# A gated linear attention and a squared-ReLU feed-forward: operand pairs of scaled float16 in place of float32r

## The chip, the cores and the metric

The kernel runs on one core of a Trainium2 chip. A core has a matrix engine (PE, with its weight loads shown apart as PEld), a vector engine (DVE), an activation engine (ACT), GpSimd (POOL) and a sync engine (SP), which here issues most DMAs. The metric is the device time of one execution in microseconds (us).

## The reference

A linear attention with a per-channel forget gate gives `x` of 3072 tokens by 384; a feed-forward with a squared ReLU takes it up to 2048 and back to 384. All in float32.

```python
f = 1.0 / (1.0 + np.exp(-f_logit))                  # B, H, S, D = 4, 8, 768, 48
for t in range(S):
    state = f[:, :, t, :, None] * state + einsum('bhd,bhe->bhde', k[:, :, t], v[:, :, t])
    y[:, :, t] = einsum('bhd,bhde->bhe', q[:, :, t], state)
x = y.transpose(0, 2, 1, 3).reshape(3072, 384)
h = x @ w_in                                        # 384 x 2048
g = np.maximum(h, 0.0) ** 2
out = g @ w_out                                     # 2048 x 384
```

## The kernel before

**Blocks.** The tokens are cut into 6 blocks of 512 (4 batches of 128 positions). For a block, the attention leaves three tiles `x[0..2]` of 128 rows by 512; each holds two parts, the value rounded to the matmul's number format and the rest. 24 units of attention (4 head pairs for each block) run ahead of the feed-forward blocks that need them.

**One feed-forward step.** The 2048 hidden rows are 16 groups `f` of 128. In step `f`, `up(f)` (L249) makes `h` in a PSUM bank `ph`: for each of 3 tiles of `x`, three matmuls of 128x128 by 512 (high by low, low by high, high by high), 9 in all. `square(f)` is three ACT instructions: ReLU (L259), square (L260), both in place, and a rounded copy `gh` (L261). `rest(f)` is one DVE instruction, `gl = ph - gh` (L266), after which the bank is free again. `down(f)` (L276) adds 9 matmuls into three PSUM banks `po`. `run` issues `up(n)`, `square(n)`, `rest(n)` and then `down(n - LAG)` with LAG = 2; the `ph` banks are two, in the last block three. So 96 steps issue 1728 matmuls of 512 columns (and 6 more for a fourth tile of the first block, `ys`).

**Order of the blocks.** Groups 0 to 7 of block 0 run first, between units of attention (the lists FIRST and SECOND, written out by hand, fix the order on every engine). Then come block 1 with all 16 groups, groups 8 to 15 of block 0, and blocks 2 to 5. `owed` is the last `down` and the eviction of the block before, done after the first `up` of the next. `hooks` hang further work at a step: decoding of weights during block 1 (`decode`: ACT copies the high halves, DVE puts the words together, ACT rounds them at L145, DVE makes the rest at L147), stages of attention for later blocks, DMA issues, and the sizes of the weights (`sizes`, L159, in blocks 2 and 3: an ACT sum of absolute values for each of the 32 weight tiles).

**Number format.** Both parts of `x`, of the weights and of `g` are float32r. Such a matmul is one instruction in the program and loads its own weights.

**The verdict.** `verdict` (L870) decides whether a general path must do the work over: it looks at the smallest decay (`low`) and at the weights' sizes (`sums`), turns the result by one PE transpose `pl` (L882) and leaves a flag, in block 4. In the last block at step 12 every engine loads the flag into a register; the branch stands after the last matmul, ahead of the last output DMAs. The general path is not taken with these inputs.

Of the kernel before, what the change touches and what calls it, by code (L numbers as in the profile page):

```python
# [42 lines left out]
LARGE = 2.0**120  # L43


LAG = 2
AHEAD = 4
# [20 lines left out]
VERDICT_AT = 12  # L68
# [15 lines left out]
class Moe:  # L84


    def __init__(self, ctx, tc, const, sums, out):
        self.tc, self.nc, self.sums, self.out = tc, tc.nc, sums, out

        self.const, self.w, self.row, self.ps, self.turns = const, {}, {}, {}, 0  # L90
        self.xs, self.w4, self.third_bank, self.heads = [], None, None, 0
# [101 lines left out]
    def hidden(self, ctx):  # L193
        self.gp = ctx.enter_context(self.tc.tile_pool(name="gp", bufs=3))
# [58 lines left out]
    def square(self, f):  # L253

        nc, ph = self.nc, self.ph[f]
        gh, gl = (
            self.gp.tile([P, NT], F32R, tag=t, name=f"{t}{self.blk}_{f}") for t in ("gh", "gl")
        )
        nc.scalar.activation(ph, ph, AF.Relu)  # L259
        nc.scalar.activation(ph, ph, AF.Square)  # L260
        nc.scalar.copy(out=gh, in_=ph)  # L261
        self.g[f] = gh, gl

    def rest(self, f):
# [15 lines left out]
    def run(self, hooks, obs=None, before=None):  # L280


        for n in range(len(self.fs) + LAG):
            if before and not obs and n == len(self.fs) + LAG - 1:
                return
            self.at = n
            if obs and n == len(self.fs):
                for e in range(NJ):
                    for f in self.fs[-LAG:]:
                        self.down(f, (e,))  # L290
                    for _, cs in tails(e):
                        self.nc.vector.tensor_copy(out=obs[e][:, cs], in_=self.po[e][:, cs])
# [15 lines left out]
            if n >= LAG:  # L308
                self.down(self.fs[n - LAG])
# [763 lines left out]
```

## Time and profile before

| | before |
|---|---|
| time, median of 3 runs (lowest to highest), us | 490.74 (490.41 to 490.92) |
| span of the profiled execution, us | 489.3 |
| PE / PEld / DVE / ACT / POOL busy, us | 471.9 / 377.5 / 248.9 / 284.3 / 29.7 |
| matmuls (as many weight loads) | 4775 |
| granted clock of PE, mean | 0.996 |

The page gives the span from the first to the last instruction; of the profiled execution no other time is given. The runs' median lies 1.4 us above the span. A busy time is the union of the instructions' stretches; matmuls overlap each other in it, so it says that PE has always something in flight, not that it streams at its full rate.

### The profile page before, as it was taken

How to read it: one execution, taken by the hardware profiler on the slowest of the kernel's cores; microseconds unless marked ns; L12 is line 12 of the kernel's file. 1: busy time of each engine (PE TensorE's matmuls, PEld its weight loads, DVE VectorE, ACT ScalarE, POOL GpSimd, SP SyncE). 2: the span in 40 equal slices, each digit the busy share in tenths (PEclk: the TensorE clock that was granted, in tenths of full speed). 3: DMA queues.
4: the chain of work that ended last, by engine and by line, in shares of the span. 5: the costliest groups of instructions: out<-in, count | busy, mean ns of one | idle time of the engine just before them, and what ended most of it. 6: DMA issues, size and time to landing. Idle time of an engine off the chain costs nothing.

```text
span 489.3 us, 11451 instructions
## 1 busy us (share of the span) xinstructions
PE 471.9 (96%) x4775; PEld 377.5 (77%) x4775; DVE 248.9 (51%) x456; ACT 284.3 (58%) x591; POOL 29.7 (6%) x66
## 2 busy tenths in 40 slices
PE   2889999999999999999999999999999999999996
PEld 2667777888788888888888788888888887888884
DVE  7999962678575365727335636434643322211112
ACT  4589874976755564656565665664745442534441
POOL 4411000000000000000000000000000000000000
PEclk9899999999999999999999999999999999999999
DMA  8888107582544525360423470134440001100002
GB/s 288 246 301 289 31 6 254 162 275 57 108 113 137 122 37 161 80 150 1 105 41 101 118 157 10 37 92 109 122 90 3 1 2 33 68 0 0 1 0 70
DMA packets 64748, 48.65 MB, mean 99 GB/s; under 512 B 46912, under 2 KB 50352, under 8 KB 64688
## 3 DMA queue, kind: packets, MB, share of 16 engines
q1 hardware_dynamic: 64096, 46.78, 34.6%
q0 software_dynamic: 448, 0.92, 0.9%
q8 instruction: 39, 0.64, 0.6%
q14 instruction: 21, 0.17, 0.1%
q10 hardware_dynamic: 144, 0.13, 0.1%
HBM read 35.22 MB, written 7.86 MB: 88 GB/s over the span
## 4 chain that ended last, share of the span: by engine, by line
PE 91%; DMA 5%; DVE 1%; ACT 1%; issue 1%; SPq 1%; POOL 0%; DVEq 0%; ACTq 0%
PE po L276 41%; PE ph L249 41%; DMA raw<-in_w_dram 3%; PE ds L561 2%; PE ds L550 2%; PE py L609 2%; DMA vn<-in_vN_dram 1%; PE ph L621 1%; PE ph L609 1%; PE py L621 1%; SPq L439 1%; DMA x<-ys 1%; DVE fkq L465 0%; ACT rx L487 0%; ACT ys L638 0%
## 5 line engine op out<-in xcount | busy, mean ns | idle before, releaser
L249 PE MATMUL ph<-x,w 128*128 128x512 f32 x864 | 218.2, 398 | 0.8 <-DVE sc L568 0.4
L249 PEld LDWEIGHTS ph<-x,w 128*128 128x128 f32 x864 | 161.6, 188 | 41.3 <-DMA x<-ys 1.2
L276 PE MATMUL po<-gh,w 128*128 128x512 f32 x576 | 180.9, 395 | 0.0
L266 DVE TENSOR_TENSOR gl<-ph,gh 128x512 fp32r<-128x512 f32 x96 | 66.4, 692 | 219.5 <-ACT gh L261 218.3
L259 ACT ACTIVATE ph<-ph 128x512 f32<-128x512 f32 x96 | 56.1, 585 | 147.6 <-PE ph L249 147.6
L276 PEld LDWEIGHTS po<-gh,w 128*128 128x128 f32 x576 | 108.3, 188 | 25.1
L276 PE MATMUL po<-gl,w 128*128 128x512 f32 x288 | 115.9, 402 | 0.0
L276 PEld LDWEIGHTS po<-gl,w 128*128 128x128 f32 x288 | 54.1, 188 | 13.9 <-DVE gl L266 0.7
L261 ACT CAST gh<-ph 128x512 fp32r<-128x512 f32 x96 | 56.4, 587 | 3.0
L260 ACT ACTIVATE ph<-ph 128x512 f32<-128x512 f32 x96 | 55.9, 582 | 3.0
L456 POOL TENSOR_SCALAR fkq<-fkq 128x8 f32<-128x8 f32 x18 | 12.3, 685 | 284.2 <-DVE fkq L451 124.3
L495 ACT COPY sx<-sp 48x208 f32<-48x208 f32 x44 | 16.1, 365 | 16.0 <-DVE sp L583 15.4
L451 DVE TENSOR_TENSOR_SCAN fkq<-fz,dr 128x520 f32<-128x520 f32 x18 | 22.2, 1232 | 2.1 <-ACT fz L446 2.1
L465 DVE TENSOR_TENSOR_SCAN fkq<-fz,dz 128x520 f32<-128x520 f32 x18 | 22.4, 1242 | 0.6
L609 PEld LDWEIGHTS py<-sc,vn 64*48 64x48 f32 (+1 forms) x384 | 16.2, 126 | 7.3 <-issue 7.3
L145 ACT CAST w<-wa 128x384 fp32r<-128x384 f32 (+1 forms) x33 | 16.6, 511 | 7.9 <-DVE wa L136 7.7
L609 PE MATMUL py<-sc,vn 64*48 64x64 f32 (+1 forms) x384 | 20.6, 222 | 0.0
L133 ACT CAST head<-raw 128x384 f16<-128x384 bf16 (+1 forms) x33 | 19.6, 628 | 1.2 <-DMA raw<-in_w_dram 1.1
L621 PE MATMUL py<-rx,sx 48*48 48x64 f32 x192 | 19.3, 215 | 0.0
L147 DVE TENSOR_TENSOR w<-wa,w 128x384 fp32r<-128x384 f32 (+1 forms) x33 | 18.0, 548 | 1.1 <-ACT w L145 0.6
L136 DVE SCALAR_TENSOR_TENSOR wa<-raw,head 128x384 int32<-128x384 int32 (+1 forms) x33 | 17.5, 548 | 1.3 <-ACT head L133 1.3
L159 ACT ACTIVATE junk<-w 128x384 f32<-128x384 f32 x32 | 16.8, 526 | 0.1
(105 smaller groups left out, 443.6 us busy)
## 6 DMA issues: line engine op xcount, KB each, us to landing
raw<-in_w_dram SPq DMA_DIRECT2D x32, 383.8 KB, 5.8
fkq<-in_fkqT_dram SPq DMA_DIRECT2D x15, 768.0 KB, 6.3
vn<-in_vN_dram SPq DMA_DIRECT2D x24, 192.0 KB, 4.0
steps<-fkq SPq DMA_DIRECT2D x48, 64.0 KB, 2.2
out_dram<-ob SPq DMA_DIRECT2D x12, 256.0 KB, 2.1
kn<-steps SPq DMA_DIRECT2D x12, 224.0 KB, 3.2
fkq<-in_fkqT_dram SPq DMA_DIRECT2D x9, 256.0 KB, 5.0
x<-ys SPq DMA_DIRECT2D x30, 64.0 KB, 2.4
```

Source lines behind the costliest of these rows:

```text
L133: nc.scalar.copy(out=self.upper(head, F16), in_=high)
L147: nc.vector.tensor_tensor(out=w[:, 1], in0=a, in1=w[:, 0].bitcast(F32), op=ALU.subtract)
L249: self.nc.tensor.matmul(self.ph[f], lhsT=w[:, i], rhs=x[:, j], start=first and n == 0, stop=last and n == 2)
L259: nc.scalar.activation(ph, ph, AF.Relu)
L260: nc.scalar.activation(ph, ph, AF.Square)
L261: nc.scalar.copy(out=gh, in_=ph)
L266: self.nc.vector.tensor_tensor(out=gl, in0=self.ph.pop(f), in1=gh.bitcast(F32), op=ALU.subtract)
L276: self.nc.tensor.matmul(po[e], lhsT=l, rhs=r, start=f == fs[0] and i == 0, stop=f == fs[-1] and i == 2,)
L451: V.tensor_tensor_scan(out=rr[:, ::-1], data0=self.fz[:, NZ * CZ : 0 : -1], data1=dr[:, ::-1], initial=0.0, op0=ALU.mult, op1=ALU.add,)
L465: V.tensor_tensor_scan(out=pp, data0=self.fz[:, : NZ * CZ], data1=dz, initial=0.0, op0=ALU.mult, op1=ALU.add)
L609: nc.tensor.matmul(self.py[c][h * C : h * C + m, b * C : (b + 1) * C], lhsT=self.vn[rows, b, h * D : h * D + m], rhs=self.sc[rows, h, b], ...
L621: nc.tensor.matmul(self.py[c][h * C : h * C + m, b * C : (b + 1) * C], lhsT=s[rows, b * D : b * D + m], rhs=q[rows], start=False, stop=b = ...
```

## The change

Both parts of `x`, of the weights and of `g` become float16. Since float16 has a narrow range, each is scaled by a power of two: `x` by 2^16 (in the attention: the scan `dr` starts from X_SCALE instead of 1, and POOL's two clamps take the factor back out of `pe`), the weights by 2^7 (in `halves`), `g` by 2^18 (in the ReLU's scale); evictions of `po` multiply by O_SCALE. The tiles of the weights keep their place and use half of it.

Float16 can overflow, so more is checked. The rounded copy in `square` also sums its row (`accum_out`) for each of the 96 steps, and `size_of` sums the squares of each of the 18 tiles of `x`, at steps 2, 3 and 4 of its block. The `gh` of group 0 of each block is kept (`first`). The verdict moves to the last block: at step 7 eight small matmuls add up `first` and one weight tile; its second half stands after the first third of the last `down`s, and the load of the flag after their last third.

In the last block LAG becomes 4, so that the last four `down`s are issued together, one output third after the other; `gh` and `gl` get 5 buffers instead of 3, and the evicted tiles `ob` get buffers of their own.

```diff
-LARGE = 2.0**120
+LARGE = 60000.0
+X_SCALE, W_SCALE, G_SCALE = 2.0**16, 2.0**7, 2.0**18
+R_SCALE = G_SCALE**0.5 / (X_SCALE * W_SCALE)
+O_SCALE = 1.0 / (G_SCALE * W_SCALE)
 LAG = 2
+LAST_LAG = 4
+GBUF = 5
-VERDICT_AT = 12
+TOP_AT = 2
+VERDICT_AT = 7
...
+    def halved(self, w):
+        return w.bitcast(F16)[:, :, :DM]
...
     def halves(self, w, a):
-        nc.scalar.copy(out=w[:, 0], in_=a)
-        yield
-        nc.vector.tensor_tensor(out=w[:, 1], in0=a, in1=w[:, 0].bitcast(F32), op=ALU.subtract)
+        if self.half:
+            nc.scalar.mul(out=w[:, 0], in_=a, mul=W_SCALE)
+            yield
+            nc.vector.scalar_tensor_tensor(
+                out=w[:, 1], in0=a, scalar=W_SCALE, in1=w[:, 0], op0=ALU.mult, op1=ALU.subtract
+            )
...
+    def size_of(self, blk, j, x):
+        n = (2 + NBLK) * NF + blk * NJ + j
+        junk = self.pers.tile([P, NT], F16, tag="x_junk", name=f"x_junk{n}")
+        self.nc.scalar.activation(junk, x[:, 0], AF.Square, scale=ROOT, accum_out=self.sums[:, n : n + 1])
...
-            self.xs[slot].tile([P, 2, NT], F32R, tag=f"x{j}", name=f"x{blk}_{j}") for j in range(NJ)
+            self.xs[slot].tile([P, 2, NT], F16 if self.half else F32R, tag=f"x{j}", name=f"x{blk}_{j}")
...
-        nc.scalar.activation(ph, ph, AF.Relu)
+        if self.half and f == 0:
+            gh = self.pers.tile([P, NT], F16, name=f"first{self.blk}")
+            self.first.append(gh)
+        nc.scalar.activation(ph, ph, AF.Relu, scale=R_SCALE if self.half else 1.0)
         nc.scalar.activation(ph, ph, AF.Square)
-        nc.scalar.copy(out=gh, in_=ph)
+        if self.half:
+            n = 2 * NF + self.blk * NF + f
+            nc.scalar.activation(gh, ph, AF.Copy, accum_out=self.sums[:, n : n + 1])
...
             if obs and n == len(self.fs):
                 for e in range(NJ):
-                    for f in self.fs[-LAG:]:
+                    for f in self.fs[-lag:]:
                         self.down(f, (e,))
+                    if e < len(ends):
+                        ends[e]()
...
-        for n in range(2):
-            hook(len(order) - 2, VERDICT_AT + n, 1, lambda: general.append(next(found)))
-        hook(
-            len(order) - 1, VERDICT_AT, 1,
-            lambda: general.append(nc.values_load(general[1][0:1, 0:1], min_val=0, max_val=1)),
+        for blk in range(NBLK):
+            for j in range(NJ):
+                hook(blk if blk > 1 else 1 - blk, TOP_AT + j, 1, lambda blk=blk, j=j: moe.size_of(blk, j, xs[blk][j]))
+        hook(len(order) - 1, VERDICT_AT, 1, lambda: next(found))
+        ends = (
+            lambda: general.append(next(found)),
+            lambda: None,
+            lambda: general.append(nc.values_load(general[0][0:1, 0:1], min_val=0, max_val=1)),
         )
...
+    for blk, first in enumerate(moe.first):
+        nc.tensor.matmul(
+            pt[:NBLK, 0], lhsT=sel[:, NBLK - blk : 2 * NBLK - blk], rhs=first,
+            start=blk == 0, stop=blk == NBLK - 1,
+        )
+    nc.tensor.matmul(pt[0:1, 1, :DM], lhsT=sel[:, NBLK : NBLK + 1], rhs=v, start=True, stop=True)
```

**PE, last block.** Before, an `up`, a `down` and the next `up` are these rows (`ph_9` is the bank of group 9, `gl_7` and `gh_7` the parts of `g` of group 7, `po_0_0` to `po_0_2` the output thirds):

```order
L249 MATMUL ph_9_5124<-x_0_4143,w_0_1336 128x512 x3
L249 MATMUL ph_9_5124<-x_1_4144,w_0_1336 128x512 x3
L249 MATMUL ph_9_5124<-x_2_4145,w_0_1336 128x512 x3
L276 MATMUL po_0_0_4930<-gl_7_5085,w_1_1100 128x512
L276 MATMUL po_0_0_4930<-gh_7_5084,w_1_1100 128x512 x2
L276 MATMUL po_0_1_4931<-gl_7_5085,w_1_1100 128x512
L276 MATMUL po_0_1_4931<-gh_7_5084,w_1_1100 128x512 x2
L276 MATMUL po_0_2_4932<-gl_7_5085,w_1_1100 128x512
L276 MATMUL po_0_2_4932<-gh_7_5084,w_1_1100 128x512 x2
L249 MATMUL ph_10_5149<-x_0_4143,w_0_1388 128x512 x3
```

Of the change, the place after step 7 of the same block: the last of six sums of a `first` tile, the sum of the weight tile `v_abs`, a product of tiny numbers, and then the `up` of group 8.

```order
L946 LDWEIGHTS sel
L946 MATMUL totals<-first_4931,sel 6x512
L950 LDWEIGHTS sel
L950 MATMUL totals<-v_abs,sel 1x384
L951 LDWEIGHTS tinies
L951 MATMUL totals<-tinies 1x1
L279 LDWEIGHTS w_0_1304
L279 MATMUL ph_8_5141<-x_0_4171,w_0_1304 128x512
```

Every float16 matmul is now two instructions, a weight load and the matmul, and the eight matmuls of the verdict stand between a `down` and the next `up`.

**DVE, the same place.** Before, only the `rest` of each step stands there:

```order
L266 TENSOR_TENSOR gl_5_5035<-ph_5_5024,gh_5_5034 128x512
L266 TENSOR_TENSOR gl_6_5060<-ph_6_5049,gh_6_5059 128x512
L266 TENSOR_TENSOR gl_7_5085<-ph_7_5074,gh_7_5084 128x512
L266 TENSOR_TENSOR gl_8_5110<-ph_8_5099,gh_8_5109 128x512
L266 TENSOR_TENSOR gl_9_5135<-ph_9_5124,gh_9_5134 128x512
```

Of the change, behind the `rest` of step 7 (`sel` is the stationary operand of the sums, `totals` their result):

```order
L304 TENSOR_TENSOR gl_7_5097<-ph_7_5086,gh_7_5096 128x512
L937 MEMSET good 128x5
L938 MEMSET sel 128x13
L939 MEMSET sel 128x1
L940 MEMSET tiny 128x1
L942 CAST tinies<-tiny 128x1
L954 TENSOR_REDUCE good<-low 128x1
L961 TENSOR_REDUCE most<-totals 6x1
```

The fills of `sel`, for which PE's sums wait, stand behind `gl_7` in DVE's order.

**ACT, start of block 1.** Before, steps 2 and 3 with the decoding of weights between them (`head`, `w`):

```order
L259 ACTIVATE ph_2_1313<-ph_2_1313 128x512
L260 ACTIVATE ph_2_1313<-ph_2_1313 128x512
L261 CAST gh_2_1323<-ph_2_1313 128x512
L145 CAST w_0_1336<-wa_1309 128x384
L133 CAST head_131<-raw_1_1240 128x384
L259 ACTIVATE ph_3_1351<-ph_3_1351 128x512
```

Of the change:

```order
L293 ACTIVATE ph_2_1315<-ph_2_1315 128x512
L294 ACTIVATE ph_2_1315<-ph_2_1315 128x512
L297 ACTIVATE gh_2_1325,sums<-ph_2_1315 128x512
L162 ACTIVATE w_0_1338<-wa_1311 128x384
L191 ACTIVATE x_junk_1350,sums<-x_0_120 128x512
L149 CAST head_131<-raw_1_1241 128x384
L293 ACTIVATE ph_3_1355<-ph_3_1355 128x512
```

The size of one tile of `x` comes in between, and the third instruction of the step also writes a sum.

## Rows read from the trace of the kernel before

**Rows 1.** The page: busy us (share) xinstructions; granted clock in 40 slices.

```profile
PE 471.9 (96%) x4775; PEld 377.5 (77%) x4775; DVE 248.9 (51%) x456; ACT 284.3 (58%) x591; POOL 29.7 (6%) x66
...
PEclk9899999999999999999999999999999999999999
```

**Rows 2.** The page: the chain that ended last, share of the span by engine.

```profile
PE 91%; DMA 5%; DVE 1%; ACT 1%; issue 1%; SPq 1%; POOL 0%; DVEq 0%; ACTq 0%
```

**Rows 3.** The chain in order of time, last block: start us, us, what.

```profile
454.99 2.11 PE ph L249 x9
457.10 2.09 PE po L276 x9
```

**Rows 4.** Groups of instructions by line and shape: xcount | busy us, mean ns | idle before.

```profile
L249 PE MATMUL ph<-x,w 128*128 128x512 f32 x864 | 218.2, 398 | 0.8 <-DVE sc L568 0.4 <-DVE gl L266 0.3
...
L249 PEld LDWEIGHTS ph<-x,w 128*128 128x128 f32 x864 | 161.6, 188 | 41.3 <-DMA x<-ys 1.2 <-ACT x L638 0.8 <-DVE gl L266 0.7
...
L261 ACT CAST gh<-ph 128x512 fp32r<-128x512 f32 x96 | 56.4, 587 | 3.0
...
L159 ACT ACTIVATE junk<-w 128x384 f32<-128x384 f32 x32 | 16.8, 526 | 0.1
...
L159 ACT ACTIVATION_READ_ACCUMULATOR junk<-w 128x1 f32 x32 | 6.2, 192 | 0.0
...
L394 DVE MEMSET fz<- 128x9 f32 x2 | 0.1, 66 | 0.0
```

**Rows 5.** Groups by line, PE alone, from 79.9 us to the end.

```profile
L249 PE MATMUL ph<-x,w 128*128 128x512 f32 x783 | 196.6, 396 | 0.3 <-DVE gl L266 0.3
L276 PE MATMUL po<-gh,w 128*128 128x512 f32 x529 | 166.2, 395 | 0.0
L276 PE MATMUL po<-gl,w 128*128 128x512 f32 x264 | 106.0, 401 | 0.0
```

**Rows 6.** Timeline of PE: start us, us, what, xcount; three stretches.

```profile
14.35 0.82 PE L715 MATMUL ph<-one 128*128 128x512 bf16 x3
...
25.20 0.81 PE L715 MATMUL ph<-one 128*128 128x512 bf16 x3
...
442.23 2.27 PE L249 MATMUL ph<-x,w 128*128 128x512 f32 x9
```

**Rows 7.** Line L715 (bfloat16 matmuls of ones): duration ns min/median/max.

```profile
L715 PE MATMUL ph<-one x8: 379/382/634, 14.4 to 25.6; 128*128 128x512 bf16 x8
...
L715 PEld LDWEIGHTS <-one x8: 96/99/118, 14.3 to 25.4; 128*128 128x128 bf16 x8
```

**Rows 8.** Windows: stretch, us, busy PE, PEld, DVE, ACT, POOL (xcount), clock, DMA.

```profile
79.90:132.00 52.10, 51.81 (x281) 41.34 (x280) 36.66 (x73) 39.41 (x76) 2.17 (x4) 1.00 0.52 158
132.00:404.00 272.00, 272.00 (x3002) 220.37 (x3000) 131.92 (x234) 157.08 (x343) 9.13 (x20) 1.00 0.35 83
```

**Rows 9.** Timeline of all engines, start of block 1: start us, us, what.

```profile
82.05 0.58 ACT L259 ACTIVATE ph<-ph 128x512 f32<-128x512 f32 x1 [1.42 <-PE ph L249]
...
83.97 0.39 PE L276 MATMUL po<-gl,w 128*128 128x512 f32 x1
...
87.17 0.58 ACT L259 ACTIVATE ph<-ph 128x512 f32<-128x512 f32 x1
...
89.02 0.69 DVE L266 TENSOR_TENSOR gl<-ph,gh 128x512 fp32r<-128x512 f32 x1 [1.15 <-ACT gh L261]
...
89.79 0.63 ACT L259 ACTIVATE ph<-ph 128x512 f32<-128x512 f32 x1
...
90.25 2.27 PE L249 MATMUL ph<-x,w 128*128 128x512 f32 x9
```

**Rows 10.** Timeline of all engines, last block, around one `rest`.

```profile
444.33 0.39 PE L276 MATMUL po<-gl,w 128*128 128x512 f32 x1
...
446.38 0.69 DVE L266 TENSOR_TENSOR gl<-ph,gh 128x512 fp32r<-128x512 f32 x1 [3.51 <-ACT gh L261]
```

**Rows 11.** Timeline of all engines, the last `down`s.

```profile
480.72 0.19 PEld L276 LDWEIGHTS po<-gl,w 128*128 128x128 f32 x1 [0.27 <-DVE gl L266]
```

More of the change, by code (lines that the diff above doesn't have):

```diff
@@ L266, in rest @@
         self.nc.vector.tensor_tensor(
-            out=gl, in0=self.ph.pop(f), in1=gh.bitcast(F32), op=ALU.subtract
+            out=gl, in0=self.ph.pop(f), in1=gh if self.half else gh.bitcast(F32), op=ALU.subtract
         )
@@ L278, in down, with run @@
                 )
-    def run(self, hooks, obs=None, before=None):
-        for n in range(len(self.fs) + LAG):
-            if before and not obs and n == len(self.fs) + LAG - 1:
+    def run(self, hooks, obs=None, before=None, lag=LAG, ends=()):
+        for n in range(len(self.fs) + lag):
+            if before and not obs and n == len(self.fs) + lag - 1:
                 return
@@ L307, in run @@
                 self.sums_of()
-            if n >= LAG:
-                self.down(self.fs[n - LAG])
+            if n >= lag:
+                self.down(self.fs[n - lag])
             for hook in hooks.get((n, 1), ()):
@@ L321, in keep, with scaled @@
         for e in range(NJ):
-            (self.nc.vector.tensor_copy if e % 2 else self.nc.scalar.copy)(out=part[e], in_=po[e])
+            self.scaled(e, part[e], po[e])
         return part
+    def scaled(self, e, out, po):
+        scale = O_SCALE if self.half else 1.0
+        if e % 2:
+            self.nc.vector.tensor_scalar(out=out, in0=po, scalar1=scale, scalar2=None, op0=ALU.mult)
+        else:
+            self.nc.scalar.mul(out=out, in_=po, mul=scale)
     def ending(self, end):
@@ L391, in fast_path @@
     V.memset(dr, 0.0)
-    V.memset(dr[:, C::CZ], 1.0)
+    V.memset(dr[:, C::CZ], X_SCALE)
     for fz in fzs:
@@ L866, in fast_path @@
                 )
-    return general[2], obs
+    return general[1], obs
 def verdict(nc, moe, low, ident, pool):
+    V = nc.vector
     flag = moe.const.tile([1, 1], I32, name="flag")
-    good = moe.const.tile([P, 2], F32, name="good")
-    nc.vector.tensor_reduce(
+    good = moe.const.tile([P, 5], F32, name="good")
+    most = moe.const.tile([P, 2], F32, name="most")
+    sel = moe.pers.tile([P, 2 * NBLK + 1], F16, name="sel")
+    v = moe.pers.tile([P, DM], F16, name="v_abs")
+    tiny = moe.const.tile([P, 1], F32, name="tiny")
@@ new lines, in verdict @@
+    tinies = moe.const.tile([P, 2], F16, name="tinies")
+    V.memset(good, 1.0)
+    V.memset(sel, 0.0)
+    V.memset(sel[:, NBLK : NBLK + 1], 1.0)
+    V.memset(tiny, TINY)
+    nc.scalar.copy(out=tinies[:, 0:1], in_=tiny)
+    V.tensor_copy(out=tinies[:, 1:2], in_=tiny)
+    nc.scalar.activation(v, moe.w[0, 1][:, 0], AF.Abs)
+    pt = pool.tile([P, 2, 512], F32, tag="ab", name="totals")
+    for blk, first in enumerate(moe.first):
+        nc.tensor.matmul(
+            pt[:NBLK, 0], lhsT=sel[:, NBLK - blk : 2 * NBLK - blk], rhs=first,
+            start=blk == 0, stop=blk == NBLK - 1,
+        )
@@ L875, in verdict @@
+    nc.tensor.matmul(pt[0:1, 1, :DM], lhsT=sel[:, NBLK : NBLK + 1], rhs=v, start=True, stop=True)
+    nc.tensor.matmul(
+        pt[0:1, 1, DM : DM + 1], lhsT=tinies[:, 0:1], rhs=tinies[:, 1:2], start=True, stop=True
+    )
+    V.tensor_reduce(
         out=good[:, 0:1], in_=low.rearrange("p u n -> p (u n)"), axis=mybir.AxisListType.X, op=ALU.min
     )
-    nc.vector.tensor_scalar(out=moe.sums, in0=moe.sums, scalar1=LARGE, scalar2=None, op0=ALU.is_lt)
-    nc.vector.tensor_reduce(out=good[:, 1:2], in_=moe.sums, axis=mybir.AxisListType.X, op=ALU.min)
@@ L879, in verdict @@
-    nc.vector.tensor_tensor(out=good[:, 0:1], in0=good[:, 0:1], in1=good[:, 1:2], op=ALU.min)
-    yield
-    pl = pool.tile([1, P], F32, tag="pk", name="pl")
-    nc.tensor.transpose(out=pl, in_=good[:, 0:1], identity=ident)
+    for n, x, least in (
+        (1, pt[:NBLK, 0], ENOUGH), (2, pt[0:1, 1, :DM], ENOUGH), (3, pt[0:1, 1, DM : DM + 1], P * TINY**2 * 0.999)
+    ):
+        rows = x.shape[0]
+        V.tensor_reduce(out=most[:rows, 1:2], in_=x, axis=mybir.AxisListType.X, op=ALU.min)
+        V.tensor_scalar(
+            out=good[:rows, n : n + 1], in0=most[:rows, 1:2], scalar1=least, scalar2=None, op0=ALU.is_ge
+        )
@@ L963, in general_path @@
     with ExitStack() as ff:
+        moe.hidden(ff)
         moe.xs = []
```

67 lines of the change are left out of this document (45 added, 22 removed).

## The prediction

> **What bounds the kernel now.** First the page's busy times: PE has something in flight for 96% of the span, the next engine, ACT, for 58% [rows 1]. Since matmuls overlap in that figure, the chain that ended last decides, and 91% of it is PE [rows 2]. In order of time the chain of the last block is nothing but groups of nine matmuls, 2.11 us for an `up` and 2.09 us for a `down` [rows 3]: 4.20 us for 18, or 233.3 ns from one matmul to the next. From 79.9 us to the end there are 783 + 529 + 264 = 1576 such matmuls [rows 5]; 1576 x 233.3 ns = 367.7 us of the 409.4 us from there to the end of the span. What is left is the small matmuls of the attention, and only 0.3 us of idle time is shown ahead of any of these groups [rows 5]. The granted clock is 1.00 through these stretches [rows 8], the 2.4 GHz level. So PE's pace for one 512-column matmul sets the time. At 2.4 GHz 512 columns take 213 ns; about 20 ns of the 233 are something else.
>
> **What a 16-bit matmul costs.** No float16 matmul is in the trace of before. The nearest rows are the matmuls of ones at L715: bfloat16, the same 128x128 by 512. Two runs of three take 0.82 and 0.81 us [rows 6], one matmul lasts 0.38 us [rows 7], so starts lie (0.82 - 0.38) / 2 = 220 ns and 215 ns apart. The same sum over nine float32r matmuls gives (2.27 - 0.40) / 8 = 234 ns [rows 4, 6]. The weight load is 188 ns for float32r [rows 4] and 99 ns for bfloat16 [rows 7]. I take 217 ns, the middle of the two runs; the bounds are 215 ns and, if the type changes nothing, 233 ns. A caution: the ones are one column read again and again, real operands are not.
>
> **The change part by part.**
>
> *Matmuls from 79.9 us on:* 1576 x (233.3 - 217) = 25.7 us less. At 215 it is 28.8, at 220 it is 21.0.
>
> *Matmuls before 79.9 us:* 1728 - 1576 = 152 of them, at most 2.5 us. There the order also waits for attention and for DMAs (5% of the chain is DMA [rows 2]). Between 0 and 2.5 I take 1.0.
>
> *Weight loads as instructions of their own:* 99 ns beside a matmul of 217 ns; taken as nothing, hidden by the matmul ahead of it. Without that cover it is the third rival.
>
> *ACT, sums in `square`:* 96 reads of the accumulator at 192 ns [rows 4] are 18.4 us; 18 sizes of `x` at most at the price of a 512-column ACT instruction, 587 ns, and a read, 18 x 0.78 = 14.0 us. ACT is busy 157.08 of 272.00 us in the long middle [rows 8], so both vanish there; if nothing covered them they would cost 32 us. The narrow place is the start of block 1, where ACT also decodes weights. ReLU 2 starts there at 87.17, though `up(2)` had ended by 83.97; its `rest` ends at 89.02 + 0.69 = 89.71 and frees the bank for `up(4)` at 90.25 [rows 9], a slack of 0.54 us. Afterwards PE is earlier by four groups (`up(2)`, `down(0)`, `up(3)`, `down(1)`) of 9 x 16.3 ns, 0.59 us, and the `rest` later by two reads, 0.38 us: PE then waits 0.4 us. Sizes of `x` fall on the next three steps, 2.3 us of ACT. If all of that delays PE the cost is 2.7 us; but ACT is busy only 39.41 of 52.10 us in this stretch [rows 8]. Of 0.4 to 2.7 I take 1.3.
>
> *The verdict's first half at step 7 of the last block:* PE comes to it one `down` after `up(7)`, at 9 x 217 ns = 1.95 us. The fill of `sel` stands behind `gl_7` on DVE. A `rest` ends 446.38 + 0.69 - 444.33 = 2.74 us after its `up` [rows 6, 10]; with a read (0.19) and four fills of 66 ns [rows 4] that is 3.2 us. So PE waits 1.25 us, and everything behind it in PE's order, `up(8)` first, waits with it. Then come six matmuls of 512 columns, one of 384 and a tiny one, 1.5 us. Together 2.75; bounds are 1.5 (no wait) and 4 (the sum of `v_abs`, 0.53 us of ACT behind `square(7)` [rows 4], also late).
>
> *The end:* with LAG 4 the last `gl` is ready long before it is used, which removes a wait of 0.27 us [rows 11]. The flag's load on DVE now stands between the evictions of the second and the last third. Its cover is the last third's 12 matmuls, 2.6 us, of which an eviction takes about 0.7; a load of over 1.9 us would come out at the end of the kernel. Taken as nothing.
>
> *Taken as nothing, too:* rounding to float16 instead of float32r on ACT and DVE (as many elements, in instructions of the same shapes), the scales, the buffers, half the bytes in `x`'s DMAs and fills. They stand beside PE's matmuls; a gain from them lies within the 2.5 us of the early part.
>
> **The sum.** 489.3 - 25.7 - 1.0 + 1.3 + 2.75 - 0.27 = 466.4 us of span. The runs' median lies 1.4 us above the span, so 467.8 us, 4.7% less than 490.74.
>
> **The rivals.**
>
> *ACT becomes the pace of block 1.* For: it starts late there already, and each step of 18 matmuls shrinks from 4.20 to 3.91 us while ACT gets 0.19 to 0.97 us more. Against: 12.7 us of idle time in that stretch [rows 8]. If some 12 steps keep their present length, 12 x 18 x 16.3 ns = 3.5 us of the gain are gone, and the early 1.0 too, in place of the 1.3: 471 us.
>
> *The type changes nothing (the other side).* If the 20 ns above the columns come from real operands or from alternating banks, and not from the number format, PE keeps 233 ns and only the verdict is added: 490.74 + 2.75 - 0.27, about 493 us, slower. It decides from 231.8 ns on, where 1576 matmuls save less than 2.5 us. Against it speak the rows of ones at 215 to 220 ns.
>
> *The weight loads come out.* Now that they are instructions of their own, each could wait for the matmul ahead of it: 213 + 99 = 312 ns, 79 ns more for 1728 matmuls, 136 us, so about 629 us. Against: the ones at L715 are such pairs of instructions too, and 215 to 220 ns leave no room for 99 ns. The Trainium skill says this against the change: its page "TensorE: Matmul & The Clock Gate", section "The mechanism", has weight loads overlap matmuls in flight only where they address other row groups of the array. By that rule the 629 us would come out; the trace disagrees already for float32r, with 188 ns of load inside 233 ns.
>
> *Much faster.* The same page, section "Back-to-back issue gap", gives a sustained 131 ns for 512 columns. By that the 1576 matmuls would save some 160 us and ACT would be the bound. No row here has 512 columns under 215 ns, so this gets no chance of its own.
>
> **How the numbers follow.** The forecast has 0.74, ACT's pace 0.12, a pace between 221 and 231 ns (473 to 489 us) 0.06, the type that changes nothing 0.06, the weight loads 0.02. The low end is 215 ns with the early gain whole and the smallest costs: 489.3 - 28.8 - 2.5 + 0.4 + 1.5 - 0.27 + 1.4 = 461. The high end is 220 ns with ACT's pace: 489.3 - 21.0 + 3.5 + 2.7 + 2.75 - 0.27 + 1.4 = 478. That holds the first two cases and part of the third, over 8 in 10; I take 462 to 478. Faster by over 0.2% (about what a measurement of this kernel can tell from no change) has 0.91, within 0.2% 0.01, slower 0.08.
>
> **What would show it.** In the profile of the changed kernel: groups of nine in the chain of 1.95 us instead of 2.10; weight loads of about 100 ns; the accumulator reads as 114 more ACT instructions of about 192 ns; PE waiting for DVE once, about 1.2 us, ahead of the line of the `totals` matmuls; ReLUs 2 to 6 of block 1 late, with waits of `up` for `gl` of some tenths. The prediction is wrong if the nine take other than 1.93 to 1.98 us, or if PE shows idle time of several us anywhere after 80 us.

## The result and the profile after

The changed kernel takes 468.91 us, the median of 4 runs (467.79 to 469.12), against 490.83 us for the kernel before in the same session: a ratio of 0.9549, 95% interval 0.9536 to 0.9563. The forecast was 467.8 us. The profiled execution has a span of 466.1 us [before: 489.3]; it took 467.79 us, the lowest of the four.

The page of the changed kernel: busy times, granted clock in 40 slices, and shares of the chain that ended last.

```profile
PE 441.0 (95%) x4781; PEld 222.6 (48%) x4783; DVE 251.3 (54%) x467; ACT 304.4 (65%) x725; POOL 28.9 (6%) x66
...
PEclk9999999999999999999999999999999999999998
...
PE 75%; ACT 8%; DVE 7%; DMA 5%; SPq 2%; issue 2%; POOL 0%; DVEq 0%
```

Beside [rows 1, 2], PE's share of the chain has dropped from 91% to 75%, and ACT and DVE have gone from 1% each to 8% and 7%: PE now waits for them somewhere. 2% is SP's sequencer. From 79.5 to 122.9 us this chain has no matmul at all; it runs through ACT, DVE, SP and DMAs.

Its chain in order of time, last block (start us, us, what), where [rows 3] had 2.11 and 2.09:

```profile
430.98 1.94 PE po L314 x9
432.92 1.94 PE ph L279 x9
```

Eighteen matmuls in 3.88 us are 215.6 ns each, from two rounded rows; over all 512-column matmuls from 130 us on, without gaps, the trace has a mean of 216.0 ns from one start to the next [before: 233.4].

Groups of the page: count, busy us and mean ns of one, idle before. They answer to [rows 4].

```profile
L279 PE MATMUL ph<-x,w 128*128 128x512 f16 x864 | 200.9, 379 | 5.0 <-DVE gl L304 4.3
...
L279 PEld LDWEIGHTS <-w 128*128 128x128 f16 x870 | 84.5, 98 | 107.7 <-issue 7.6
...
L297 ACT ACTIVATION_READ_ACCUMULATOR gh<-ph 128x1 f32 x90 | 17.5, 194 | 0.0
```

A weight load takes 98 ns and nothing is seen of it on PE. But PE now stands idle for 4.3 us ahead of `up`, for `gl` on DVE, 4.1 us of it after 77 us. Where that is, the timeline of PE in block 1 says (only rows with idle time in brackets; a fourth, of 0.19 us, is at 87.4; the view ends at 124, so the last row has five of its nine matmuls):

```profile
112.33 2.10 PE L279 MATMUL ph<-x,w 128*128 128x512 f16 x9 [1.37 <-DVE gl L304]
...
116.73 2.10 PE L279 MATMUL ph<-x,w 128*128 128x512 f16 x9 [0.35 <-DVE gl L304]
...
122.96 1.24 PE L279 MATMUL ph<-x,w 128*128 128x512 f16 x5 [2.19 <-DVE gl L304]
```

`gl` is late since its ReLU is. The timeline of ACT ahead of two of these places shows the ReLU (L293) right behind a rounding of weights (L162) that had waited for `wa`:

```profile
109.21 0.52 ACT L162 ACTIVATE w<-wa 128x384 f16<-128x384 f32 x1 [2.20 <-DVE wa L152]
109.64 0.58 ACT L293 ACTIVATE ph<-ph 128x512 f32<-128x512 f32 x1
...
119.84 0.52 ACT L162 ACTIVATE w<-wa 128x384 f16<-128x384 f32 x1 [2.21 <-DVE wa L152]
120.27 0.58 ACT L293 ACTIVATE ph<-ph 128x512 f32<-128x512 f32 x1
```

And the timeline of DVE shows what `wa` (L152) had stood behind: a scan and a multiply of an attention unit, which `hooks` put between the decoding steps.

```profile
117.37 1.24 DVE L519 TENSOR_TENSOR_SCAN fkq<-fz,dz 128x520 f32<-128x520 f32 x1
118.65 0.69 DVE L522 TENSOR_TENSOR fkq<-fkq 128x512 f32<-128x512 f32 x1
119.26 1.02 DVE L152 SCALAR_TENSOR_TENSOR wa<-raw,head 128x384 int32<-128x384 int32 x2
```

The kernel before had the same waits. ACT's waits for `wa` in block 1 up to 132 us (in total, times, longest), first before and then after:

```profile
ACT w L145 <- DVE wa L136: 7.1, 6, 2.4
```

```profile
ACT w L162 <- DVE wa L152: 6.7, 5, 2.2
```

But then ACT had caught up with PE in between: its ReLUs at 100.96 and 105.16 waited for PE, and the slack took the next wait up.

```profile
100.96 0.58 ACT L259 ACTIVATE ph<-ph 128x512 f32<-128x512 f32 x1 [0.18 <-PE ph L249]
...
105.16 0.58 ACT L259 ACTIVATE ph<-ph 128x512 f32<-128x512 f32 x1 [0.91 <-PE ph L249]
```

Now that PE is faster and ACT has more to do, it does not catch up: the ReLU of the `up` that ends by 108.85 starts at 112.86.

```profile
112.86 0.62 ACT L293 ACTIVATE ph<-ph 128x512 f32<-128x512 f32 x1
```

The timeline of PE at step 7 of the last block, the place of the second term of the forecast:

```profile
417.99 0.59 PE L314 MATMUL po<-gh,w 128*128 128x512 f16 x2
419.54 1.46 PE L946 MATMUL totals<-first,sel 128*6 128x512 f16 x6 [0.95 <-DVE tiny L940]
...
421.09 2.12 PE L279 MATMUL ph<-x,w 128*128 128x512 f16 x9
```

A wait for DVE and, from 419.54 to 421.09, 1.55 us of small matmuls stand between two groups of nine.

The end. The last matmul starts at 484.09 of 489.3 us before and at 459.85 of 466.1 us after: 5.2 us then, 6.24 us now. First the branch, by its line (count, duration ns, first and last start), then the evicted tiles and their DMAs:

```profile
L1092 SPq EVENT_SEMAPHORE  x8: 17/17/17, 459.3 to 459.8; - x8
...
L1092 SPq COMPARE_BRANCH  x1: 45/45/45, 456.6 to 456.6; - x1
```

```profile
L332 DVE TENSOR_SCALAR ob_last<-po x4: 415/547/691, 455.6 to 460.6; 128x512 f32<-128x512 f32 x2, 128x256 f32<-128x256 f32 x2
L1101 SPq DMA_DIRECT2D out_dram<-ob_last x3: 332/340/372, 460.0 to 461.0; - x3
L1101 ACTq DMA_DIRECT2D out_dram<-ob_last x1: 378/378/378, 460.7 to 460.7; - x1
...
DMA to landing us min/median/max: 2.6/3.9/4.0
```

SP branches at 456.6 and issues nothing until 459.3, 2.6 us later. The thirds whose evictions start at 455.6 and 457.7 wait for that, and all three go out within 1 us. From the issue of such a DMA to its landing (its end in the trace) the median is 3.9 us. In the kernel before, where SP had branched at 422.3, the same line is

```profile
DMA to landing us min/median/max: 2.1/2.5/2.9
```

### The profile page after: what moved, and what is told of

Its sections match the earlier page's. It is cut to its first block, busy times and chain, and to the rows that moved or that the text cites. A ratio compares the mean times of both kernels' runs of the same rounds, so it can differ in the third digit from the quotient of the medians.

```text
span 466.1 us, 11546 instructions
## 1 busy us (share of the span) xinstructions
PE 441.0 (95%) x4781; PEld 222.6 (48%) x4783; DVE 251.3 (54%) x467; ACT 304.4 (65%) x725; POOL 28.9 (6%) x66
## 4 chain that ended last, share of the span: by engine, by line
PE 75%; ACT 8%; DVE 7%; DMA 5%; SPq 2%; issue 2%; POOL 0%; DVEq 0%
PE po L314 34%; PE ph L279 33%; DMA raw<-in_w_dram 2%; PE ds L615 2%; DMA fkq<-in_fkqT_dram 2%; PE ds L604 2%; ACT ph L294 2%; ACT gh L297 1%; ACT ph L293 1%; PE py L663 1%; ACT w L162 1%; DVE wa L152 1%; ACT head L149 1%; DVE fkq L519 1%; PE ph L675 1%
## 5 line engine op out<-in xcount | busy, mean ns | idle before, releaser
L279 PE MATMUL ph<-x,w 128*128 128x512 f16 x864 | 200.9, 379 | 5.0 <-DVE gl L304 4.3
L314 PE MATMUL po<-gh,w 128*128 128x512 f16 x540 | 160.6, 379 | 0.0
L304 DVE TENSOR_TENSOR gl<-ph,gh 128x512 f16<-128x512 f32 x90 | 62.1, 690 | 170.3 <-ACT gh L297 170.1
L279 PEld LDWEIGHTS <-w 128*128 128x128 f16 x870 | 84.5, 98 | 107.7 <-issue 7.6
L314 PEld LDWEIGHTS <-w 128*128 128x128 f16 x864 | 82.9, 98 | 98.8 <-issue 0.4
L293 ACT ACTIVATE ph<-ph 128x512 f32<-128x512 f32 x96 | 56.1, 584 | 103.1 <-PE ph L279 103.1
L314 PE MATMUL po<-gl,w 128*128 128x512 f16 x288 | 109.4, 380 | 0.1
L297 ACT ACTIVATE gh<-ph 128x512 f16<-128x512 f32 x90 | 53.7, 597 | 2.8
L507 POOL TENSOR_SCALAR fkq<-fkq 128x8 f32<-128x8 f32 x18 | 12.7, 706 | 268.6 <-DVE fkq L503 177.6
L162 ACT ACTIVATE w<-wa 128x384 f16<-128x384 f32 (+1 forms) x33 | 16.8, 515 | 7.9 <-DVE wa L152 7.4
L675 PE MATMUL py<-rx,sx 48*48 48x64 f32 x192 | 19.6, 216 | 0.1
L152 DVE SCALAR_TENSOR_TENSOR wa<-raw,head 128x384 int32<-128x384 int32 (+1 forms) x33 | 17.6, 547 | 2.9 <-ACT head L149 2.9
L164 DVE SCALAR_TENSOR_TENSOR w<-wa,w 128x384 f16<-128x384 f32 (+1 forms) x33 | 18.0, 548 | 1.6 <-ACT w L162 1.1
L297 ACT ACTIVATION_READ_ACCUMULATOR gh<-ph 128x1 f32 x90 | 17.5, 194 | 0.0
L663 PE MATMUL ph<-sc,vn 64*48 64x64 f32 (+1 forms) x256 | 16.6, 222 | 0.0
```

The source lines that it names most:

```text
L152: nc.vector.scalar_tensor_tensor(out=a.bitcast(I32), in0=low, scalar=13, in1=head.bitcast(I32), op0=ALU.logical_shift_right, op1=ALU.bitwi ...
L279: self.nc.tensor.matmul(self.ph[f], lhsT=w[:, i], rhs=x[:, j], start=first and n == 0, stop=last and n == 2)
L293: nc.scalar.activation(ph, ph, AF.Relu, scale=R_SCALE if self.half else 1.0)
L297: nc.scalar.activation(gh, ph, AF.Copy, accum_out=self.sums[:, n : n + 1])
L304: self.nc.vector.tensor_tensor(out=gl, in0=self.ph.pop(f), in1=gh if self.half else gh.bitcast(F32), op=ALU.subtract)
L314: self.nc.tensor.matmul(po[e], lhsT=l, rhs=r, start=f == fs[0] and i == 0, stop=f == fs[-1] and i == 2,)
```

## The experiments

Times are medians; each ratio is to the kernel before, run in the same session.

| run | us | ratio, 95% interval |
|---|---|---|
| the change | 468.91 | 0.9549 (0.9536 to 0.9563) |
| e1_no_sums | 467.03 | 0.9534 (0.9494 to 0.9574) |
| e1b_no_x_sizes | 467.15 | 0.9511 (0.9494 to 0.9527) |
| e2_late_sizes | 467.32 | 0.9513 (0.9497 to 0.9529) |
| e3_early_fill | 467.02 | 0.9523 (0.9503 to 0.9543) |
| e4_early_out | 469.37 | 0.9572 (0.9556 to 0.9588) |
| e6_lag2 | 470.81 | 0.9580 (0.9557 to 0.9603) |
| e7_slots | 474.38 | 0.9672 (0.9652 to 0.9692) |
| e9_no_verdict | 464.38 | 0.9442 (0.9418 to 0.9467) |
| e10_best | 465.87 | 0.9481 (0.9462 to 0.9499) |
| e11_type_alone | 461.90 | 0.9399 (0.9375 to 0.9423) |

### Where the 17 ns of a matmul come from

**m1_pace:** matmuls alone, in stretches of 36, with a number format, a width of the stationary operand and a number of columns for each.

> Leaves the whole computation out: twelve stretches of 36 matmuls each on the matrix engine alone, with real gate logits as operands, float32r or float16, and 128, 96, 64 or 32 stationary columns against 512, 256 or 128 moving columns. Theory A: the 233 ns of a float32r matmul are set by its weight load (188 ns plus a gap), so they shrink with the stationary columns: 233 ns at 128, about 216 at 96, 64 and 32; and with 256 moving columns float32r stays above 200 ns while float16 goes to about 110. Rival B: the 20 ns above the columns come with the four-byte moving operand: float32r stays at 233 ns for 96, 64 and 32 stationary columns, and goes to some 120 to 130 ns at 256 moving columns, or to the 188 ns of the load. Both: float16 at 216 ns for 128x512.

The timeline of PE (start us, us, what; a row runs over several stretches where only shapes change):

```profile
24.28 7.94 PE L1100 MATMUL bank<-h,h 128*128 128x512 f16 x36
...
61.30 8.24 PE L1100 MATMUL bank<-h,h 128*128 128x256 f16 x108
```

Groups of matmuls and of weight loads with float32r, 128 and 32 stationary columns (xcount | busy us, mean ns | idle before):

```profile
L1100 PE MATMUL bank<-r,r 128*128 128x512 f32 x72 | 17.0, 394 | 0.0
L1100 PE MATMUL bank<-r,r 128*32 128x512 f32 x36 | 8.5, 394 | 0.0
...
L1100 PEld LDWEIGHTS bank<-r,r 128*128 128x128 f32 x108 | 17.9, 188 | 3.2
L1100 PEld LDWEIGHTS bank<-r,r 128*32 128x32 f32 x36 | 3.9, 109 | 4.4
```

The theory that the weight load sets 233 ns fell. From start to start (medians of the trace) a float32r matmul takes 227 ns with 128 stationary columns (its load 188 ns), 230 with 96 (161 ns), 230 with 64 (134 ns) and 232 with 32 (109 ns): the load shrinks and the matmul doesn't. With 256 moving columns it is 120 ns against 109 for float16, with 512 it is 227 against 216. So about 11 ns stay with the format of the matmul, whatever it loads and at both lengths; this is the rival's shape, though not its 233 ns. What in the format costs them is not shown. The last row of the timeline shows loads hidden even where matmuls are shorter than they: 108 matmuls in 8.24 us, 76 ns each on average, while a float16 load has a mean of 101 to 110 ns in that run.

**m2_pace:** the kernel's pattern of nine, one to nine moving tiles, all ones as data, and DVE and ACT reading PSUM beside it.

> Measures matmuls alone and leaves the whole computation out (the outputs hold two PSUM banks): stretches of 36 matmuls of 128x128 by 512 in the kernel's pattern of nine for each bank. In order: float16 with one moving tile; float32r with one; float16 with nine moving tiles; float32r with nine; float32r, all ones, one tile; float32r with DVE and ACT reading another PSUM bank beside it; float32r with three moving tiles; float16 with nine tiles and DVE and ACT reading PSUM beside; float32r the same; float32r; float16. Known from the run before: 215.8 ns for float16, 227.4 ns for float32r, while the kernel shows 216.0 and 233.3 ns. Theory A (the other 6 ns of float32r are PSUM or SBUF traffic of DVE and ACT beside it): 233 ns only in the two busy float32r stretches, float16 stays at 216. Theory B (they come from changing moving tiles): 233 ns with three and nine tiles, 227 with one. Theory C (data): ones below 227 ns. If all float32r stretches show 227 ns the 6 ns stay open.

Its timeline of PE, the stretches of ones, of DVE and ACT beside it together with three moving tiles (x72), and the last one:

```profile
51.47 8.32 PE L1106 MATMUL bank<-cx,cw 128*128 128x512 f32 x36
59.63 16.48 PE L1106 MATMUL bank<-rx,rw 128*128 128x512 f32 x72
...
106.12 7.94 PE L1106 MATMUL bank<-hx,hw 128*128 128x512 f16 x36
```

(8.32 - 0.39) / 35 = 226.6 ns for ones, (16.48 - 0.39) / 71 = 226.6 ns with traffic and with three tiles; the median with nine tiles is 227 ns too, and float16 has 216 ns throughout. None of the three theories holds. The 6 ns by which float32r is slower in the kernel (233) than alone (227) stay unexplained. The traces show one more thing about them: several float32r stretches of both runs start with up to ten matmuls of 224 to 240 ns before they settle at 226 to 227, and in the kernel nearly all lie between 228 and 238 and never settle. The result rests on 233 against 216 as rows show them in the kernels themselves, not on this.

### Block 1

**e1_no_sums** leaves out the row sums of `gh` and the sizes of `x`; **e1b_no_x_sizes** only the latter; **e2_late_sizes** leaves nothing out and moves block 1's sizes of `x` to block 2.

Of e1; e1b has only the first of these two edits:

```diff
-        junk = self.pers.tile([P, NT], F16, tag="x_junk", name=f"x_junk{n}")
-        self.nc.scalar.activation(junk, x[:, 0], AF.Square, scale=ROOT, accum_out=self.sums[:, n : n + 1])
+        pass
...
-            nc.scalar.activation(gh, ph, AF.Copy, accum_out=self.sums[:, n : n + 1])
+            nc.scalar.activation(gh, ph, AF.Copy)
```

Of e2:

```diff
-                hook(blk if blk > 1 else 1 - blk, TOP_AT + j, 1, lambda ...)
+                k, n = (2, TOP_AT + 4 + j) if blk == 1 else (blk or 1, TOP_AT + j)
+                hook(k, n, 1, lambda ...)
```

> Leaves out the row sums of the squares and the sizes of x (range checks that do not enter the output). Theory A: the waits of the matrix engine in block 1 (5.0 us of idle time ahead of the up matmuls in the changed kernel) come from the activation engine's added work: they fall under 1 us and the time by 4 us, to about 465. Rival B: the faster matmuls alone used up the slack that block 1 had, and the activation engine waits there for the vector engine anyway: the waits stay at 3 us or more and the time falls by less than 2 us, to 467 or more.

> Leaves out the sizes of x alone (a range check that does not enter the output); the row sums of the squares stay. Theory A: of the added work in block 1 the sizes of x are 2.4 us and the reads of the accumulator about 2.3 us (12 steps by 0.19), so about half of the 4 us: time about 467. Rival B: below 1 us of difference, 468 or more.

> The whole computation and all checks; only the sizes of block 1's x move from steps 2 to 4 of block 1 to steps 6 to 8 of block 2. Theory A: as without the sizes of x, since the other blocks hide them: about 467. Rival B: no difference that can be measured against the changed kernel, about 469.

PE's waits for `gl` in e1, of which the longest is the one near 120 us (us, times, longest):

```profile
PE ph L278 <- DVE gl L303: 2.3, 2, 2.1
```

The wait of 1.4 us near 112 us is 0.1 us without the sizes of `x` and not there when they come later: it belongs to them, and moving them is worth 0.0036 of the ratio, 1.8 us. The last wait stays in all three, 2.1 to 2.2 us of PE time, in e1 with no added ACT work in block 1 at all. So the added ACT work makes the smaller waits only; the large one comes with PE's pace and with what stands ahead of `wa` on DVE. In these three profiles a second cost follows it, the clock (last section), which eats part of what is saved. By time, e1b and e2 came out as their theory A said. e1 came out as neither of its two: 2.1 us of waits are left after 77 us, and its interval holds the change's own ratio, so its time alone shows nothing.

**e7_slots** moves the attention units 8 and 9, whose scans stand ahead of `wa`, two and three steps later.

```diff
-SLOTS = (12, 14, 19, 21, 22, 28, 31, ...
+SLOTS = (14, 17, 19, 21, 22, 28, 31, ...
```

> The changed kernel, but the attention units 8 and 9 stand two and three steps later in the feed-forward of block 1 (slots 14 and 17 instead of 12 and 14). Theory (ACT is held by decode's words, which stand on DVE behind those units' K and Q stages): the waits of up for gl at 110 to 121 us (in sum 4.4 us, the last one 2.35 us) leave that place; since decoding goes on to step 14, at most one of 1 to 2.4 us comes back about 8 to 12 us later. Sum of block 1's waits 1 to 3 us instead of 4.75, time 1.5 to 3.5 us less. Rival (ACT's pace alone, with its more and faster steps, whatever stands on DVE): the waits stay at 110 to 121 us, in sum 4 to 5 us, time the same within 0.7 us.

In block 1 the waits of `up` are 0.85 us in sum from start to start, where the changed kernel has 4.75: the theory holds for their cause. The forecast of the time missed: it got 5.5 us worse. The waits of the stretch from 137 to 160 us (engine, line, waited for; us, times, longest):

```profile
PE ph L279 <- DVE x L697: 8.4, 1, 8.4
DVE fkq L503 <- ACT fz L498: 8.1, 1, 8.1
ACT fz L498 <- DMA fkq<-in_fkqT_dram: 7.8, 1, 7.8
```

Unit 9 now stands right ahead of unit 10, whose input arrives 7.8 us late on ACT; DVE's scan waits for ACT and PE for DVE. SP issues that input's DMA only at 145.1 us, after waiting 9.6 us for matmuls of the attention (L675). Behind the wait, from 154.3 to 159.4 us, the clock was at 0.50, the 1.2 GHz level, and the next nine matmuls took 4.00 us. The order of the queues has one wait taken out and a longer one put in.

### The verdict and the end

**e3_early_fill** issues the fills of the selector at step 4 and leaves the eight small matmuls at step 7.

```diff
+        hook(len(order) - 1, VERDICT_AT - 3, 1, lambda: next(found))
         hook(len(order) - 1, VERDICT_AT, 1, lambda: next(found))
...
     nc.scalar.activation(v, moe.w[0, 1][:, 0], AF.Abs)
+    yield
```

> The changed kernel, but the first part of the verdict (fill of the selector, the tiny number, the absolute values of one weight tile) is issued at step 4 of the last block instead of step 7; the eight small matmuls stay at step 7. Theory (the prediction's: matmul of the sums waits only because the fills stand behind the DVE part of step 7): the 1.1 us of PE idle time ahead of the sums goes, the sums still take about 1.6 us, the stretch from the last matmul of down(5) in that step to up(8) shrinks from about 4.8 to about 3.7 us, the time falls by about 1.1 us. Rival (the sums wait for the last first-group tile or a semaphore of ACT, not for the fills): the wait stays at about 1 us and nothing is gained.

The timeline of PE at that place, now without idle time:

```profile
418.75 0.59 PE L314 MATMUL po<-gh,w 128*128 128x512 f16 x2
419.28 1.46 PE L948 MATMUL totals<-first,sel 128*6 128x512 f16 x6
```

The wait went as its theory has it, and the ratio is 0.0026 lower, 1.3 us; the two intervals overlap (0.9543 against 0.9536), so it is the timeline that shows the gain, and the time agrees with it.

**e9_no_verdict** leaves the verdict out; the flag is a constant, loaded at step 12.

> The changed kernel with the whole verdict left out: no sums of the kept tiles, no second half; the flag is a constant that is written at step 7 of the last block and loaded at step 12, as early as in the kernel before. Theory (the verdict costs twice: 1.1 us of waiting and 1.6 us of small matmuls at step 7, and 1.05 us at the end since SP's branch comes late): no PE wait and no extra matmuls ahead of up(8), the stretch from the last matmul's start to the end of the span back from 6.2 to about 5.2 us, the time 3.5 to 3.9 us less, about 465.1 us. Rival (the end grew for another cause, the scaled evictions or the order of the thirds): the stretch stays at 6.2 us, the time only 2.7 us less, about 466.2 us.

Its evicted tiles and their DMAs:

```profile
L1102 SPq DMA_DIRECT2D out_dram<-ob_last x3: 332/333/341, 455.0 to 460.2; - x3
...
DMA to landing us min/median/max: 2.0/2.1/2.3
```

The thirds go out as they are evicted, from 455.0 on, and land in 2.1 us instead of 3.9. From the last matmul's start to the end it is 4.50 us: shorter than the 5.2 that was expected. LAG 4 spreads the thirds 2.6 us apart, and with LAG 2 and no verdict (e11, below) it is 5.25. The late branch, with the verdict's second half ahead of it, thus costs 6.24 - 4.50 = 1.74 us; LAG 4 by itself takes 0.7 off, and 1.05 is left of the two. The time fell by 4.5 us (5.3 by the ratios), more than expected; the profile does not account for all of it.

**e4_early_out** issues the first two thirds' DMAs on SP ahead of its flag load.

```diff
-            lambda: None,
-            lambda: general.append(nc.values_load(general[0][0:1, 0:1], min_val=0, max_val=1)),
+            lambda: nc.sync.dma_start(out[NBLK - 1, 0:P], obs_of[0][0]),
+            lambda: (
+                nc.sync.dma_start(out[NBLK - 1, P : 2 * P], obs_of[0][1]),
+                general.append(nc.values_load(general[0][0:1, 0:1], min_val=0, max_val=1)),
+            ),
...
```

> The changed kernel, but the output DMAs of the first and second third of the last block are issued on SP as soon as each is evicted, ahead of SP's load of the flag and its branch; the last third's two halves go out behind the branch, both on ACT's queue. Theory (the end got longer by 1.05 us since SP's first instruction behind its branch comes some 2.6 us after the branch, and three thirds then go out at once): the first two thirds' DMAs are issued about 456.8 and 459 us, the last lands by about 463.6 us, and the stretch from the last matmul to the end of the span falls from 6.2 to about 5.2 us; time about 1 us less. Rival (the landing of the last third alone sets the end, however the others go): the stretch stays within 0.3 us of 6.2.

Both theories missed: the stretch became 7.0 us. By the branch's line and the DMAs',

```profile
L1096 SPq EVENT_SEMAPHORE  x8: 17/17/17, 462.9 to 463.4; - x8
...
L1096 SPq COMPARE_BRANCH  x1: 45/45/45, 460.3 to 460.3; - x1
```

```profile
L1104 ACTq DMA_DIRECT2D out_dram<-ob_last x2: 378/382/385, 463.5 to 464.0; - x2
...
DMA to landing us min/median/max: 2.2/2.4/3.3
```

the transfers land fast again, but SP's flag load stands behind its second DMA, its branch comes at 460.3 instead of 456.6, and ACT's last DMAs come out at 463.5, behind SP's first instruction after the branch. That fewer thirds were in flight (landing in 2.4 us instead of 3.9) did not make up for a branch that came 3.7 us later.

**e6_lag2** sets `LAST_LAG` from 4 back to 2.

> The changed kernel with LAG 2 in the last block, all else kept. Theory (four downs together are the cover of the verdict's second half, of the flag's loads and of the time that SP takes from its branch to its next instruction): thirds are 1.3 us instead of 2.6, the flag comes some 1.3 us nearer to the last matmul, the stretch from there to the end grows from 6.2 to about 7.5 us, and PE waits 0.3 to 1 us for the last gl: the time 1.5 to 2.5 us more, about 471 us. Rival (LAG 4 is worth only the 0.27 us wait of the kernel before): about 469.2 us.

The time is as expected, 1.9 us more by the medians, and PE waits 0.3 us for the last `gl`; but the stretch is 9.2 us and not 7.5, and the profiled span 3.3 us longer than that of the change. SP branches at 459.6 and goes on at 462.4, after the last matmul's start at 460.2, and all DMAs go out from 463.0 to 464.0:

```profile
L1101 SPq DMA_DIRECT2D out_dram<-ob_last x3: 341/372/1949, 463.1 to 464.0; - x3
L1101 ACTq DMA_DIRECT2D out_dram<-ob_last x1: 1282/1282/1282, 463.0 to 463.0; - x1
...
DMA to landing us min/median/max: 4.0/4.2/5.0
```

### The type alone, and the best version

**e11_type_alone** is the formats and scales without any of the new checks: no row sums, no sizes of `x`, no verdict (the flag is a constant), and LAG 2.

> The number formats and scales of the change alone: the row sums in square, the sizes of x and the verdict are left out (the flag is a constant written at step 7 and loaded at step 12), and LAG is 2 in the last block as before. Theory (the gain is PE's pace from 79.9 us on, 27 us, and 2.4 us ahead of it; the losses are the checks and the waits of block 1): 490.8 - 27.2 - 2.4 + 2.4 to 4.5 (waits of block 1 and the slower clock behind them) = 463.6 to 465.7 us. Rival (part of the gain comes from the moved verdict and LAG 4 and not from the type): over 467 us.

461.90 us, 1.7 us below the expected range: the type is worth more than the whole gain, and the checks, with LAG 4, take back 0.9549 - 0.9399 = 1.5% of 490.8 us, 7 us. The stretch at the end is 5.25 us, that of the kernel before.

**e10_best** leaves nothing out. It has e2's and e3's moves, and the second half of the verdict ahead of the last of the four `down`s of the first third instead of behind it.

```diff
                     for f in self.fs[-lag:]:
+                        if ends and e == 0 and f == self.fs[-1]:
+                            ends[-1]()
                         self.down(f, (e,))
...
```

> The changed kernel with three moves and nothing left out: block 1's sizes of x come in block 2, the fills of the verdict come three steps earlier, and the second half of the verdict stands ahead of the last of the four downs of the first output third instead of behind it. Theory: the 1.5 us wait at 110 us and the 1.1 us wait ahead of the sums go, the flag is ready some 0.6 us earlier relative to the last matmul and the end gets shorter by as much: about 3 us less, 465.8 us; if PE falls to half clock behind the 2.35 us wait that stays, about 1.5 us of that is lost. Rival (each saved wait comes back at the next one): within 1 us of 468.9.

465.87 us (465.23 to 466.72), as expected, and the fastest measured version that computes everything: its interval lies below that of the change. The wait ahead of the sums is gone and the waits of `up` in block 1 are 3.0 us of idle time instead of 4.1; the end is 5.97 us, 0.3 shorter instead of 0.6. These three parts are 2.5 us from start to start (1.1 + 1.1 + 0.3), where the theory had 3; that the time came out so close is in part luck.

## Why the prediction was right, step by step

**The signs.** The nine matmuls of the chain take 1.94 us, a weight load 98 ns, and ACT has 114 more reads of the accumulator (194 ns for those of `gh`), all as forecast. One sign came out against the prediction: it called itself wrong if PE showed idle time of several us anywhere after 80 us, and PE shows 4.1 us in block 1. By that sign the step on block 1 was wrong, though the time lies in the range.

**Matmuls.** "217 ns, the middle of the two runs": it is 216.0 ns, near the lower bound. 1576 x (233.4 - 216.0) = 27.4 us instead of 25.7. That the ones at L715 could stand for real operands held.

**Matmuls before 79.9 us.** The first matmul of the same `up` starts at 77.34 instead of 79.75: 2.4 us instead of 1.0, near the upper end; in the other profiles with everything computed it lies between 77.0 and 78.7. Where these 2.4 us come from was not tested. Between 20 and 25 us the mean clock was 0.66 in the kernel before and 1.00 in the changed one; but e1 and e11 have 0.66 there too, and start at 76.4 and 77.5.

**Weight loads.** Taken as nothing, and nothing it is: 98 ns inside 216.0. The rule of the Trainium skill behind that rival ("TensorE: Matmul & The Clock Gate", "The mechanism"), by which loads overlap only matmuls in other row groups, does not describe these full-array pairs; m1 shows 76 ns for a matmul with a load longer than that.

**ACT backlog in block 1.** This step failed in size: 1.3 us were taken, with 2.7 as the bound, and PE's idle time ahead of `up` grew from 0.3 [rows 5] to 4.1 us after 77 us; from start to start, beyond the pace, it grew from 0.47 to 4.75 us, by 4.3. The working followed ACT's own durations through the first steps, where 0.2 us of waiting came as predicted, and then trusted ACT's idle time, 12.7 us of 52 [rows 8]. Of this, 7.1 us were no reserve: ACT was waiting in order for DVE's `wa`, which stood behind attention. e1 and e11 show that the largest wait needs none of the added ACT work, e7 that it leaves with the attention units; e2 gives 1.8 us of the rest to the sizes of `x`. The rival "ACT becomes the pace of block 1" had the place and the size (3.5 us), but ACT is not busy all through: it waits 6.7 us for `wa`. What sets the time there is the order of ACT and DVE together: the chain that ended last has no matmul from 79.5 to 122.9 us.

**Verdict at step 7.** Predicted 1.25 + 1.5 us; from start to start 1.12 us of waiting and 1.55 us of matmuls, 2.67 in all. e3 removed the wait by moving the fills, which shows what it was.

**The end.** "Taken as nothing" failed: 1.05 us. The step looked at the flag's load on DVE (543 ns, hidden as forecast) and not at what follows a load on every other engine, the branch. SP takes 2.6 us from its branch to its next instruction. e9 puts the late branch at 1.74 us. LAG 4 was credited with 0.27 us, but [rows 11] is a row of the weight load: of that wait the next matmul starts show 0.1 us on PE (0.33 instead of 0.23 us). What LAG 4 does save is at the output: 0.7 us without the late branch (e11 and e9), and with it the 3 us by which the stretch is longer in e6.

**The sum.** -27.4 - 2.4 + 4.3 + 2.7 + 1.05 = -21.8 us, against -23.2 us between the two spans. Most of the rest is in a place that the prediction has no term for: in the kernel before, behind each of 17 bursts of attention after 120 us, the second matmul of the feed-forward starts 0.33 to 0.34 us after the first, 0.1 us more than the pace, 1.8 us in sum; in the changed kernel it does not, but one burst, at 136 us, takes 0.6 us longer. The forecast's span, 466.4 us, came out so close to 466.1 by luck in part: the gains were taken some 4 us too small (matmuls, the time before 79.9 us, the place just named), and so were the costs (block 1, the end, the wait that LAG 4 removes). From span to time the prediction added 1.4 us, where single runs on record take 1.7 us; its 467.8 us met the profiled run, the fastest of the four, and the median is 1.1 us above it.

## What to carry to other kernels

When the bounding engine gets faster, idle time of the next engine is a reserve only if that engine is not waiting, in its order, for a third one; read what ended each idle stretch before counting on it. A branch or a flag moved towards the end of a program brings with it the time from the branch to the next instruction on the engines that still have work to issue, here 2.4 to 3.0 us on SP and ACT where the branch came late. A bound from a row of the same instruction shape, 215 to 220 ns from matmuls of ones, held here although its data were unlike the kernel's.

## What was not expected of the hardware

**A matmul of float32r costs more whatever its load:** 227 against 216 ns for 128x512, 120 against 109 ns for 128x256 (m1), and 233 against 216 in the kernels.

**The clock fell after a wait of 2.2 us, but not always.** Windows of e9_no_verdict, then of the changed kernel, around the same wait (us, busy PE, PEld, DVE, ACT, POOL with counts, clock, DMA share, GB/s):

```profile
118.00:123.60 5.60, 3.65 (x17) 1.56 (x16) 4.15 (x8) 3.33 (x9) 0.00 (x0) 1.00 0.37 88
123.60:127.00 3.40, 3.16 (x8) 1.16 (x8) 3.25 (x6) 2.59 (x6) 0.00 (x0) 0.51 0.15 24
```

```profile
122.70:126.00 3.30, 3.04 (x73) 1.78 (x72) 3.17 (x6) 3.21 (x8) 0.00 (x0) 1.00 0.11 19
```

After 2.19 us of idle PE in both, the clock is at 0.51, the 1.2 GHz level, in the one and stays at the 2.4 GHz level in the other. The first nine matmuls take 3.69 us there instead of 2.10. So this wait cost 1.6 us more than its length. The clock fell there in four profiles (e1, e1b, e2, e9) and did not in six with the same wait; what decides was not found, and part of the scatter of these runs may come from it.

**A branch was followed by 2.5 to 2.9 us without an instruction on SP,** in every profile of the whole kernel and wherever the branch stood: 422.3 to 425.0 in the kernel before, 456.6 to 459.3 in the changed kernel, 460.3 to 462.9 in e4, 459.6 to 462.4 in e6, 455.2 to 458.1 in e10. The Trainium skill ("Runtime: NRT & Kernel Launch", "Instruction fetch mechanics") says that a taken branch out of the fetched window waits until its target is fetched by DMA. The length is near that of a DMA (2.1 us from issue to landing in e9), but no run here separates fetching from other causes.
